# A gate accumulator moved from a PSUM bank to its own SBUF tile, with the freed bank given to the pool of products and convolution

## The chip, the cores and the metric

The kernel runs on one core of one Trainium2 chip. The metric is the device time of one execution in microseconds. The engines that matter here are PE (matrix multiply, output to PSUM only), DVE (vector), ACT (scalar and copies), POOL (elementwise on SBUF) and SP (issues most of the DMAs). All engines run their own instruction streams in order and wait for each other by semaphores. PSUM has eight banks of 512 float32 values on each of 128 partitions; SBUF is the large on-chip memory that all the other tiles lie in.

## The reference

```python
# x: (8, 4224, 192); weight: (8 heads, 7 taps); conv_w: (5, 192); w_val, w_out: (192, 192)
w = softmax(weight)                              # per head, over its 7 taps
x = causal_depthwise_conv(x, w)                  # 7 taps, one filter for each group of 24 channels
gate_pre = sum(conv_w[k] * xp[:, k:k+S] for k in range(5))   # causal, a filter for each channel
gate = 1 / (1 + exp(-gate_pre))
out = (gate * (x @ w_val)) @ w_out
```

Everything is float32.

## The kernel before

Channels lie on partitions and tokens along the free axis. 192 channels don't fit in 128 partitions, so the two halves of the batch are processed side by side in three chunks: chunks 0 and 1 hold 128 channels of each half (tile `x1`, 128 x 2 x m), and chunk 2 holds the remaining 64 channels of both halves (tile `x2`, 128 x m). The tokens are cut into 36 steps of up to m = 502 tokens (24 of them have 502, eight have 448).

The first convolution is done on PE against a banded matrix (`conv_unit`, line 312), copied out of PSUM by ACT (line 321) and rearranged by DMAs into `x1` and `x2`. For each step n the main loop (lines 571 to 598) then does this:

- **The gate.** `gate_open` (ACT, line 382) writes the first of the five taps into an accumulator; `gate_taps` (DVE, line 389) adds four more, each in place: accumulator = x * tap + accumulator; `gate_close` (ACT, line 402) takes the sigmoid. Chunks 0 and 1 share a two-bank PSUM accumulator `pa` (up to 1004 values a partition), chunk 2 has a one-bank PSUM accumulator `pb` (up to 502). The sigmoids go to the SBUF tiles `g1` and `g2`. The profile calls both of these `g`.
- **The first product.** `diagonal`, `main`, `columns` and `rows` (lines 445, 455, 483, 468) form v = x @ w_val in three PSUM banks taken from the pool `ps`.
- **Gating.** `gated` (DVE, line 502) multiplies v from PSUM by the gate, into `g1` or `g2`.
- **Splitting.** To multiply float32 at speed, each operand is split in a rounded part and a remainder: `split1` and `split2` (ACT casts in lines 410 and 418, POOL subtractions in lines 411 and 419). They make `xh`, `xl` from x, and `ph`, `pl` from the gated product. POOL's `pl` of line 411 is that of chunks 0 and 1, and that of line 419 is chunk 2's.
- **The second product** has the same functions with "o", and `project` (ACT, line 518) copies it out.

The pool `ps` serves the products and the banded convolution: five banks before, beside two for `pa` and one for `pb`, which are all eight. The order of instructions on every engine is written out by hand: it is the order of the calls in the loop. In a step DVE does the last two `pa` taps of gate n+1, gating of chunk 2 of step n, gating of chunks 0 and 1, the four `pb` taps of gate n+1, and the first two `pa` taps of gate n+2. POOL does `xl` of step n+1 (lines 411, 419), then `pl` of chunk 2 (line 419) and of chunks 0 and 1 (line 411) of step n.

Of the kernel before, what the change touches and what calls it, by code (L numbers as in the profile page):

```python
# [7 lines left out]
F32 = mybir.dt.float32  # L8
# [5 lines left out]
PSUM = bass.MemoryType.PSUM  # L14
# [62 lines left out]
MB = 502  # L77
# [22 lines left out]
def kernel(  # L100
# [16 lines left out]
    gp = ctx.enter_context(tc.tile_pool(name="gp", bufs=2))  # L117
    pp = ctx.enter_context(tc.tile_pool(name="pp", bufs=2))
    op = ctx.enter_context(tc.tile_pool(name="op", bufs=3))
    ps_g = ctx.enter_context(tc.tile_pool(name="ps_g", bufs=1, space=PSUM))  # L120
    ps_h = ctx.enter_context(tc.tile_pool(name="ps_h", bufs=1, space=PSUM))
    ps = ctx.enter_context(tc.tile_pool(name="ps", bufs=5, space=PSUM))
    ctx.enter_context(
        tc.manual_schedule(engines={ENG.PE, ENG.Activation, ENG.DVE, ENG.Pool, ENG.SP})
    )
# [237 lines left out]
    def views(n, k=KG - 1):  # L363
        g, o, m = STEPS[n]
        b = second(NJS[g])
        x1v = x1s[g][:, : 2 * b].rearrange("p (a t) -> p a t", a=2)
        return x1v[:, :, o + k : o + k + m], x2s[g][:, o + k : o + k + m]
# [3 lines left out]
    accs, g1s, g2s, xs, pr, ots, banks = {}, {}, {}, {}, {}, {}, {}  # L371

    def gate_open(n, i):
        if n >= N:
            return
        m = STEPS[n][2]
        if i == 0:
            acc = ps_g.tile([128, 2, 512], F32, tag="pa", name=f"pa_{n}")[:, :, :m]
        else:
            acc = ps_h.tile([128, 512], F32, tag="pb", name=f"pb_{n}")[:, :m]  # L380
        accs[n, i] = acc
        nc.scalar.mul(acc, views(n, 0)[i], cwt[:, i, 0:1])  # L382

# [10 lines left out]
    def gate_close(n, i):  # L394
        if n >= N:
            return
        m = STEPS[n][2]
        if i == 0:
            dst = g1s[n] = gp.tile([128, 2, MB], F32, tag="g1", name=f"g1_{n}")[:, :, :m]
        else:  # L400
            dst = g2s[n] = gp.tile([128, MB], F32, tag="g2", name=f"g2_{n}")[:, :m]
        nc.scalar.activation(dst, accs.pop((n, i)), AF.Sigmoid)  # L402


# [150 lines left out]
    conv(3)  # L555
    zeros(WARM[2])
    gate_open(0, 0)
    gate_open(0, 1)
    split(0)
    w_out.join(nc.gpsimd)  # L560
    gate_taps(0, 0)
    conv(1)
    gate_close(0, 0)
    gate_open(1, 0)
    w_out.cast(nc.gpsimd)
    conv(first_unit[LAG] - done[0])
    gate_taps(0, 1)
    gate_close(0, 1)
    gate_open(1, 1)

    for n in range(N + 1):
        diagonal("v", n)
        gate_taps(n + 1, 0, 1, 3)
        split(n + 1)
        diagonal("o", n - 1)
        main("v", n, 0)
        main("v", n, 1)
        gate_taps(n + 1, 0, 3, KG)
        columns("v", n)
        gated(n, 2)  # L580
        gate_close(n + 1, 0)
        gate_open(n + 2, 0)
        columns("o", n - 1)
        split_gated2(n)
        project(n - 1, 2)
        rows("v", n)
        gated(n, 0)
        gated(n, 1)
        rows("o", n - 1)
        split_gated1(n)  # L590
        main("o", n - 1, 0)
        gate_taps(n + 1, 1)
        project(n - 1, 0)
        main("o", n - 1, 1)
        project(n - 1, 1)
        conv(todo[n])
        gate_close(n + 1, 1)
        gate_open(n + 2, 1)
# [90 lines left out]
```

## Time and profile before

| | |
|---|---|
| median of 3 runs (range) | 393.77 us (392.7 to 394.51) |
| profiled execution, its own time | 391.79 us |
| span of the profiled execution, first to last instruction | 390.0 us |
| mean granted clock of PE | 0.990 |
| HBM read and written | 29.34 MB, 26.00 MB |

The profiled execution lies 0.5% under the median, and 1.79 us of its time lie outside the span. A "busy" PE in these tables need not be at its peak, since matmuls are pipelined and their ends are modelled. In a row of groups the columns are: line, engine, operation, output and inputs by the program's names, partitions x elements, count, then busy time and mean duration of one in ns, then the idle time of the engine just ahead of these instructions and what ended it. A row of a timeline has start and length in us; "x4" there is four instructions in a row, with the length from the first one's start to the last one's end.

### The profile page before, as it was taken

How to read it: one execution, taken by the hardware profiler on the slowest of the kernel's cores; microseconds unless marked ns; L12 is line 12 of the kernel's file. 1: busy time of each engine (PE TensorE's matmuls, PEld its weight loads, DVE VectorE, ACT ScalarE, POOL GpSimd, SP SyncE). 2: the span in 40 equal slices, each digit the busy share in tenths (PEclk: the TensorE clock that was granted, in tenths of full speed). 3: DMA queues.
4: the chain of work that ended last, by engine and by line, in shares of the span. 5: the costliest groups of instructions: out<-in, count | busy, mean ns of one | idle time of the engine just before them, and what ended most of it. 6: DMA issues, size and time to landing. Idle time of an engine off the chain costs nothing.

```text
span 390.0 us, 8633 instructions
## 1 busy us (share of the span) xinstructions
PE 377.6 (97%) x3204; PEld 322.4 (83%) x3204; DVE 343.5 (88%) x432; ACT 323.7 (83%) x525; POOL 254.6 (65%) x178
## 2 busy tenths in 40 slices
PE   8778999999999999999999999999999999999895
PEld 8768989988888888888888888888888777888684
DVE  5897797888998998998999899899899999999971
ACT  5668798988888888888889888888888888887873
POOL 1968665566667665666666676666566776776781
PEclk9988999999999999999999999999999999999999
DMA  8876779998787688777767768758887644334223
GB/s 301 227 194 206 210 222 281 248 278 258 251 248 217 180 258 248 220 216 244 236 188 242 229 191 260 210 184 265 251 231 218 224 153 154 115 119 151 81 106 145
DMA packets 38226, 82.49 MB, mean 212 GB/s; under 512 B 4841, under 2 KB 17513, under 8 KB 38185
## 3 DMA queue, kind: packets, MB, share of 16 engines
q1 hardware_dynamic: 36936, 80.06, 66.7%
q0 software_dynamic: 960, 1.39, 1.5%
q8 instruction: 25, 0.41, 0.5%
q10 hardware_dynamic: 288, 0.50, 0.4%
q14 instruction: 17, 0.13, 0.1%
HBM read 29.34 MB, written 26.00 MB: 142 GB/s over the span
## 4 chain that ended last, share of the span: by engine, by line
PE 78%; DVE 11%; DMA 4%; ACT 3%; issue 2%; SPq 0%; POOL 0%; DVEq 0%; ACTq 0%
PE pc L312 22%; PE o L455 11%; PE v L455 10%; PE v L483 7%; PE v L468 6%; PE o L483 6%; PE o L468 5%; DVE pa L389 5%; PE v L445 5%; PE o L445 5%; DVE pb L389 3%; DMA x<-xw 3%; DVE g L502 2%; PE pw L204 1%; DMA x<-e 1%
## 5 line engine op out<-in xcount | busy, mean ns | idle before, releaser
L389 DVE SCALAR_TENSOR_TENSOR pa<-x,cwt,pa 128x1004 f32<-128x1004 f32 (+5 forms) x144 | 172.9, 1201 | 5.1 <-ACT pa L382 1.3
L411 POOL TENSOR_TENSOR xl<-x,xh 128x1004 fp32r<-128x1004 f32 (+5 forms) x36 | 74.7, 2075 | 75.4 <-ACT xh L410 67.8
L312 PEld LDWEIGHTS pc<-band,x 128*120 128x120 f32 x912 | 103.3, 187 | 8.4 <-DMA x<-xw 3.6
L312 PE MATMUL pc<-band,x 128*120 128x122 f32 x912 | 104.8, 272 | 5.3 <-DMA x<-xw 5.3
L389 DVE SCALAR_TENSOR_TENSOR pb<-x,cwt,pb 128x502 f32<-128x502 f32 (+5 forms) x144 | 102.3, 710 | 3.8
L502 DVE TENSOR_TENSOR g<-v,g 128x502 f32<-128x502 f32 (+5 forms) x108 | 66.0, 643 | 24.3 <-PE v L468 16.2
L411 POOL TENSOR_TENSOR pl<-g,ph 128x1004 fp32r<-128x1004 f32 (+5 forms) x36 | 79.3, 2201 | 8.3 <-ACT ph L410 6.4
L402 ACT ACTIVATE g<-pa 128x1004 f32<-128x1004 f32 (+5 forms) x36 | 34.5, 958 | 41.9 <-DVE pa L389 20.3
L419 POOL TENSOR_TENSOR pl<-g,ph 128x502 fp32r<-128x502 f32 (+5 forms) x36 | 42.9, 1191 | 37.0 <-ACT ph L418 37.0
L321 ACT COPY e<-pc 120x488 f32<-120x488 f32 x114 | 59.2, 588 | 6.1 <-PE pc L312 5.8
L518 ACT COPY ot<-o 128x502 f32<-128x502 f32 (+5 forms) x108 | 55.8, 551 | 1.2 <-PE o L455 0.7
L382 ACT ACTIVATE pa<-x,cwt 128x1004 f32<-128x1004 f32 (+5 forms) x36 | 37.8, 1050 | 6.7 <-DMA x<-e 4.9
L419 POOL TENSOR_TENSOR xl<-x,xh 128x502 fp32r<-128x502 f32 (+5 forms) x36 | 41.8, 1162 | 0.1
L483 PEld LDWEIGHTS v<-x,wvf 128*64 128x64 f32 x576 | 29.0, 136 | 11.8 <-issue 11.4
L483 PE MATMUL v<-x,wvf 128*64 128x126 f32 (+5 forms) x576 | 37.1, 270 | 0.0
L410 ACT CAST ph<-g 128x1004 fp32r<-128x1004 f32 (+5 forms) x36 | 35.1, 976 | 1.2 <-DVE g L502 1.2
L483 PE MATMUL o<-g,wof 128*64 128x126 f32 (+5 forms) x576 | 35.5, 264 | 0.0
L410 ACT CAST xh<-x 128x1004 fp32r<-128x1004 f32 (+5 forms) x36 | 34.6, 962 | 0.0
L483 PEld LDWEIGHTS o<-g,wof 128*64 128x64 f32 x576 | 30.8, 136 | 0.1
L455 PE MATMUL o<-ph,woh 128*128 128x502 f32 (+5 forms) x72 | 30.8, 428 | 0.0
L455 PE MATMUL v<-xh,wvl 128*128 128x502 f32 (+5 forms) x72 | 27.1, 376 | 0.0
L455 PE MATMUL v<-xh,wvh 128*128 128x502 f32 (+5 forms) x72 | 27.0, 376 | 0.0
(75 smaller groups left out, 574.7 us busy)
## 6 DMA issues: line engine op xcount, KB each, us to landing
x<-xw SPq DMA_DIRECT2D x64, 300.0 KB
out<-ot SPq DMA_DIRECT2D x24, 753.0 KB
x<-e SPq DMA_DIRECT2D x40, 285.9 KB
x<-xw SPq DMA_DIRECT2D x20, 360.0 KB
out<-ot SPq DMA_DIRECT2D x8, 672.0 KB
x<-e SPq DMA_DIRECT2D x32, 141.6 KB
x<-e SPq DMA_DIRECT2D x25, 171.6 KB
x<-e SPq DMA_DIRECT2D x16, 94.4 KB
```

Of the source, the lines that this page charges most:

```text
L312: nc.tensor.matmul(pc[:M, k * WIN : (k + 1) * WIN], lhsT=xtiles[i][:, c : c + M], rhs=band[:, 4 * q + hi, :], start=True, stop=True,)
L321: nc.scalar.copy(e[:, a : a + w], pc[:M, :w])
L389: nc.vector.scalar_tensor_tensor(out=acc, in0=views(n, k)[i], scalar=cwt[:, i, k : k + 1], in1=acc, op0=ALU.mult, op1=ALU.add,)
L410: nc.scalar.copy(h, x)
L411: nc.gpsimd.tensor_tensor(out=l, in0=x, in1=h.bitcast(F32), op=ALU.subtract)
L419: nc.gpsimd.tensor_tensor(out=l, in0=x, in1=h.bitcast(F32), op=ALU.subtract)
L445: nc.tensor.matmul(acc, lhsT=a[:, r], rhs=b, start=(i == 0), stop=False)
L455: nc.tensor.matmul(acc, lhsT=a[:, r], rhs=b[:, q], start=(fresh and i == 0), stop=(not fresh and i == 2))
L468: nc.tensor.matmul(acc, lhsT=a[p, r], rhs=b[p], start=(fresh and i == 0), stop=(not fresh and i == 2))
L483: nc.tensor.matmul(acc[p, c], lhsT=w.f[:, W12 : W12 + 64], rhs=x[:, q, c], start=False, stop=(i == 3),)
L502: nc.vector.tensor_tensor(out=v, in0=banks.pop(("v", n, q)), in1=v, op=ALU.mult)
L518: nc.scalar.copy(ots[n][:, q * m : (q + 1) * m], banks.pop(("o", n, q)))
```

## The change

Chunk 2's gate is no longer summed in a PSUM bank. `gate_open` allocates `g2` itself in SBUF and writes the first tap there, `gate_taps` adds the other four in place in that tile, and the sigmoid of `gate_close` runs in place. The pool of one bank for `pb` goes, and the pool `ps` has six banks. `pa` stays in PSUM.

```diff
-    ps_h = ctx.enter_context(tc.tile_pool(name="ps_h", bufs=1, space=PSUM))
-    ps = ctx.enter_context(tc.tile_pool(name="ps", bufs=5, space=PSUM))
+    ps = ctx.enter_context(tc.tile_pool(name="ps", bufs=6, space=PSUM))
...
         if i == 0:
             acc = ps_g.tile([128, 2, 512], F32, tag="pa", name=f"pa_{n}")[:, :, :m]
         else:
-            acc = ps_h.tile([128, 512], F32, tag="pb", name=f"pb_{n}")[:, :m]
+            acc = gp.tile([128, MB], F32, tag="g2", name=f"g2_{n}")[:, :m]
         accs[n, i] = acc
         nc.scalar.mul(acc, views(n, 0)[i], cwt[:, i, 0:1])
...
         if i == 0:
             dst = g1s[n] = gp.tile([128, 2, MB], F32, tag="g1", name=f"g1_{n}")[:, :, :m]
         else:
-            dst = g2s[n] = gp.tile([128, MB], F32, tag="g2", name=f"g2_{n}")[:, :m]
+            dst = g2s[n] = accs[n, i]
         nc.scalar.activation(dst, accs.pop((n, i)), AF.Sigmoid)
```

No instruction is added or removed, and on no engine does one change its place: all five streams are the same but for the tile names and the waits (and line numbers, which are one lower). Three things differ in the waits. The pool `gp` has two buffers of `g2`, and the buffer is now taken when the gate is opened, not when it is closed, so ACT's opening of chunk 2 waits for POOL's subtraction (line 419) on the gate two before, where it waited for nothing but ACT itself; gating no longer waits for POOL in chunk 2; and PE waits for other releases of banks, since there are six to go round.

ACT before, at the end of step 7 (closing of chunk 2 of gate 8, opening of gate 9, the casts of x, closing and opening of chunks 0 and 1):

```order
L402 ACTIVATE g2_8_1366<-pb_8_1249 128x502 [waits DVE_49]
L382 ACTIVATE pb_9_1368<-x2_4_817,cwt_156 128x502 [waits Activation_49]
L410 CAST xh_9_1376<-x1_4_816 128x1004
L418 CAST xh2_9_1380<-x2_4_817 128x502
L402 ACTIVATE g1_9_1407<-pa_9_1290 128x1004 [waits DVE_49,PE_49,Pool_49]
L382 ACTIVATE pa_10_1409<-x1_4_816,cwt_156 128x2x502 [waits Activation_49]
```

The same place after:

```order
L401 ACTIVATE g2_8_1238<-g2_8_1238 128x502 [waits DVE_49]
L381 ACTIVATE g2_9_1356<-x2_4_810,cwt_153 128x502 [waits Pool_49]
L409 CAST xh_9_1364<-x1_4_809 128x1004
L417 CAST xh2_9_1368<-x2_4_810 128x502
L401 ACTIVATE g1_9_1395<-pa_9_1279 128x1004 [waits DVE_49,PE_49,Pool_49]
L381 ACTIVATE pa_10_1397<-x1_4_809,cwt_153 128x2x502 [waits Activation_49]
```

Nothing moved; the opening of chunk 2 waits for POOL, and both operands of the closing are one SBUF tile.

DVE before, in step 8 (the taps of chunk 2, the taps of chunks 0 and 1 and the gating that follows them):

```order
L389 SCALAR_TENSOR_TENSOR pb_9_1368<-x2_4_817,cwt_156,pb_9_1368 128x502 [waits Activation_49]
L389 SCALAR_TENSOR_TENSOR pb_9_1368<-x2_4_817,cwt_156,pb_9_1368 128x502 [waits DVE_49] x3
L389 SCALAR_TENSOR_TENSOR pa_10_1409<-x1_4_816,cwt_156,pa_10_1409 128x2x502 [waits Activation_49]
L389 SCALAR_TENSOR_TENSOR pa_10_1409<-x1_4_816,cwt_156,pa_10_1409 128x2x502 [waits DVE_49] x3
L502 TENSOR_TENSOR g2_9_1499<-v_9_2_1503,g2_9_1499 128x502 [waits PE_49,Activation_49,Pool_49]
```

The same place after:

```order
L388 SCALAR_TENSOR_TENSOR g2_9_1356<-x2_4_810,cwt_153,g2_9_1356 128x502 [waits Activation_49]
L388 SCALAR_TENSOR_TENSOR g2_9_1356<-x2_4_810,cwt_153,g2_9_1356 128x502 [waits DVE_49] x3
L388 SCALAR_TENSOR_TENSOR pa_10_1397<-x1_4_809,cwt_153,pa_10_1397 128x2x502 [waits Activation_49]
L388 SCALAR_TENSOR_TENSOR pa_10_1397<-x1_4_809,cwt_153,pa_10_1397 128x2x502 [waits DVE_49] x3
L501 TENSOR_TENSOR g2_9_1356<-v_9_2_1490,g2_9_1356 128x502 [waits PE_49,Activation_49]
```

The four taps of chunk 2 now read both their tensors from SBUF and write to SBUF; the taps of chunks 0 and 1 still have theirs in PSUM.

## The prediction

> **What bounds the kernel now.** I read the busy times first, then the chain that ended last, the busy times by stretch, one step of the timeline, and the waits. From the page:
>
> ```profile
> PE 377.6 (97%) x3204; PEld 322.4 (83%) x3204; DVE 343.5 (88%) x432; ACT 323.7 (83%) x525; POOL 254.6 (65%) x178
> ...
> PE 78%; DVE 11%; DMA 4%; ACT 3%; issue 2%; SPq 0%; POOL 0%; DVEq 0%; ACTq 0%
> PE pc L312 22%; PE o L455 11%; PE v L455 10%; PE v L483 7%; PE v L468 6%; PE o L483 6%; PE o L468 5%; DVE pa L389 5%; PE v L445 5%; PE o L445 5%; DVE pb L389 3%; DMA x<-xw 3%; DVE g L502 2%; PE pw L204 1%; DMA x<-e 1%
> ```
>
> PE carries 78% of the chain, DVE 11%, of which the taps of chunk 2 (`pb`) are 3%. By stretch (columns: stretch, length, busy time of PE, weight loads, DVE, ACT, POOL with counts, then clock and DMA):
>
> ```profile
> 0.00:40.00 40.00, 33.47 (x274) 31.90 (x275) 30.82 (x66) 27.36 (x53) 27.04 (x42) 0.91 0.77 227
> 40.00:100.00 60.00, 60.00 (x556) 53.56 (x556) 51.05 (x62) 50.99 (x87) 37.33 (x25) 1.00 0.87 256
> 100.00:200.00 100.00, 100.00 (x836) 84.98 (x837) 92.36 (x106) 88.01 (x139) 65.98 (x39) 1.00 0.73 222
> 200.00:300.00 100.00, 100.00 (x845) 84.35 (x845) 92.35 (x104) 86.62 (x136) 64.75 (x38) 1.00 0.77 231
> 300.00:345.00 45.00, 44.53 (x348) 35.70 (x345) 43.58 (x52) 39.31 (x61) 31.57 (x20) 1.00 0.46 153
> 345.00:390.00 45.00, 39.62 (x354) 31.95 (x353) 33.37 (x47) 31.44 (x56) 27.97 (x19) 0.99 0.35 130
> ```
>
> In the middle PE has no idle time that the profile shows, and DVE is 92% busy: a step is PE's, and DVE has about 0.8 us to spare in each 10.3 us. From 300 on DVE is busier (97%) and the chain passes through it. So whatever lengthens DVE's work in a step by more than 0.8 us sets the step. One step, on DVE and then on POOL:
>
> ```profile
> 164.32 3.08 DVE L389 SCALAR_TENSOR_TENSOR pb<-x,cwt,pb 128x502 f32<-128x502 f32 x4
> 167.30 5.17 DVE L389 SCALAR_TENSOR_TENSOR pa<-x,cwt,pa 128x1004 f32<-128x1004 f32 x4
> 172.38 0.68 DVE L502 TENSOR_TENSOR g<-v,g 128x502 f32<-128x502 f32 x1
> 173.46 1.27 DVE L502 TENSOR_TENSOR g<-v,g 128x502 f32<-128x502 f32 x2 [0.41 <-PE v L468]
> 174.65 3.08 DVE L389 SCALAR_TENSOR_TENSOR pb<-x,cwt,pb 128x502 f32<-128x502 f32 x4
> ```
>
> ```profile
> 162.78 1.28 POOL L419 TENSOR_TENSOR xl<-x,xh 128x502 fp32r<-128x502 f32 x1
> 165.06 1.26 POOL L419 TENSOR_TENSOR pl<-g,ph 128x502 fp32r<-128x502 f32 x1 [1.00 <-ACT ph L418]
> 166.52 2.33 POOL L411 TENSOR_TENSOR pl<-g,ph 128x1004 fp32r<-128x1004 f32 x1 [0.21 <-ACT ph L410]
> 171.03 2.15 POOL L411 TENSOR_TENSOR xl<-x,xh 128x1004 fp32r<-128x1004 f32 x1 [2.18 <-ACT xh L410]
> ```
>
> The reader should see the coincidence: the four `pb` taps (164.32 to 167.40) run while POOL does chunk 2's `pl` (165.06 to 166.32) and starts the large one (166.52). It recurs in every step, because `pl` can begin only when the gating just ahead of the taps is done.
>
> **The change, part by part.**
>
> *The taps get shorter.* The nearest rows: a tap with its accumulator in PSUM, and DVE operations with both tensors in SBUF, all of them from the setup.
>
> ```profile
> L389 DVE SCALAR_TENSOR_TENSOR pb<-x,cwt,pb 128x448 f32<-128x448 f32 x32 | 22.0, 687 | 0.8
> L389 DVE SCALAR_TENSOR_TENSOR pb<-x,cwt,pb 128x502 f32<-128x502 f32 x96 | 71.3, 743 | 2.6
> L389 DVE SCALAR_TENSOR_TENSOR pa<-x,cwt,pa 128x1004 f32<-128x1004 f32 x96 | 121.6, 1267 | 2.5
> L283 DVE TENSOR_TENSOR wvl<-wvf,wvh 128x448 fp32r<-128x448 f32 x1 | 0.6, 625 | 0.7 <-ACT wvh L282 0.7
> L229 DVE TENSOR_TENSOR band<-band,rs 128x488 f32<-128x488 f32 x2 | 1.3, 667 | 1.0 <-ACT band L221 1.0
> ```
>
> At 448 elements SBUF alone takes 625 ns against 687: 62 ns less. The slope is the same, (667 - 625)/40 = 1.05 ns an element against (1267 - 743)/502 = 1.04. So 144 taps save 144 x 0.062 = 8.9 us of DVE, and a step's four 0.25 us.
>
> *The sixth bank.* What PE waited for a bank in all: ahead of `v` in line 445, for ACT's copy out.
>
> ```profile
> PEld v L445 <- ACT ot L518: 0.2, 1, 0.2
> ```
>
> The bank is worth 0.2 us at the most. I take nothing: PE's rows have no gap in the middle for it to fill.
>
> *ACT.* A 502-element copy takes 578 ns out of PSUM (`ot`) and a cast 597 to 606 ns out of SBUF (`ph`, `xh`), so the sigmoid out of SBUF may cost some 30 ns more, 36 x 0.03 = 1.1 us in all. Writing the first tap to SBUF is bounded by the same 30 ns, up or down. ACT has 66 us idle in the span and lies on 3% of the chain; taken at nothing, at worst 2 us. The new wait of ACT for POOL ends early: chunk 2's `pl` of that buffer ends at 166.32, and ACT opens the next gate at 169.26, behind the closing, which itself waits for the last tap.
>
> ```profile
> L518 ACT COPY ot<-o 128x502 f32<-128x502 f32 x72 | 39.0, 578 | 0.0
> L418 ACT CAST ph<-g 128x502 fp32r<-128x502 f32 x24 | 14.3, 597 | 0.0
> L418 ACT CAST xh<-x 128x502 fp32r<-128x502 f32 x24 | 14.6, 606 | 0.0
> 169.26 0.68 ACT L382 ACTIVATE pb<-x,cwt 128x502 f32<-128x502 f32 x1
> ```
>
> *Two engines that read SBUF twice.* This is the price that decides, and no row shows it. Today a DVE tap in the loop reads one tensor from SBUF and one from PSUM, and POOL doesn't disturb it: taps beside POOL and taps without it average 687, 743 and 1267 ns for 448, 502 and 1004 elements, which lie on one line. The last DVE operation with two SBUF tensors ends in the setup before POOL's first subtraction starts:
>
> ```profile
> 15.77 0.56 DVE L249 SCALAR_TENSOR_TENSOR scr<-scr,scr 128x384 f32<-128x384 uint32 x1
> 18.52 0.84 POOL L419 TENSOR_TENSOR xl<-x,xh 128x304 fp32r<-128x304 f32 x1
> ```
>
> After the change there are four such DVE operations in each step, just beside `pl`. What the rows say of the paths: DVE takes two values from SBUF in 1.05 ns, so it has two ways in, and with a PSUM accumulator it needs only one of them. POOL needs (2339 - 1258)/502 = 2.15 ns for each element of two inputs, 1.08 ns a value: the rate of one way in.
>
> ```profile
> L411 POOL TENSOR_TENSOR pl<-g,ph 128x1004 fp32r<-128x1004 f32 x24 | 56.1, 2339 | 5.0 <-ACT ph L410 3.7 <-DMA x<-e 0.6 <-PE pc L312 0.6
> L419 POOL TENSOR_TENSOR pl<-g,ph 128x502 fp32r<-128x502 f32 x24 | 30.2, 1258 | 25.9 <-ACT ph L418 25.9
> ```
>
> The lower bound is no cost: the paths are separate, and DVE only gains 8.9 us. The upper bound is that DVE's second way in and POOL's one are the same and go to one instruction at a time, from its start to its end. I take that end, since it is the reading in which the numbers fit one shared path (a PSUM accumulator leaves POOL untouched, POOL has exactly one path's rate), and keep the other for the range.
>
> The Trainium skill, "SBUF — State Buffer", section "Who interferes with whom", says that a DVE instruction with two SBUF inputs contends with a GpSimd instruction that reads SBUF, that the shared pair is an exclusive lock, and that whichever starts second "fully blocks" until the first is done. No run here shows it yet; by that rule the sum is the one below, and without it the sum ends some 87 us lower.
>
> *The sum.* In a step of 502: the taps start. Tap 2 ends, and `pl` of chunk 2, ready 0.7 us after the taps began, goes first: tap 3 waits 1.26 us. By then ACT has cast chunks 0 and 1, so the large `pl` is ready, and in the gap after tap 3 it goes ahead of tap 4: 2.33 us. POOL's `xl` doesn't collide, because its casts stand on ACT behind the closing of chunk 2, which waits for the last tap; it has the 5.08 us of `pa` taps and the gating to finish. DVE's step is then 2.98 - 0.25 (167.30 - 164.32, less the saving) + 5.08 (172.38 - 167.30) + 0.68 + 1.19 (174.65 - 173.46) = 9.68 us of work and 3.59 of waiting: 13.27 us against 10.33 (174.65 - 164.32). PE (10.33) and ACT (under 10) then have slack, and DVE no longer waits for PE.
>
> ```profile
> L411 POOL TENSOR_TENSOR pl<-g,ph 128x1004 fp32r<-128x1004 f32 (+5 forms) x36 | 79.3, 2201 | 8.3 <-ACT ph L410 6.4
> L419 POOL TENSOR_TENSOR pl<-g,ph 128x502 fp32r<-128x502 f32 (+5 forms) x36 | 42.9, 1191 | 37.0 <-ACT ph L418 37.0
> ```
>
> For the whole span: all `pl` is 122.2 us; the last step's 1.9 us (a small block, no taps beside it) don't count, which leaves 120.3. DVE's busy time 343.5 - 8.9 + 120.3 = 454.9. DVE's idle time between 40 and 345 (305 - 279.3 = 25.7 us) is swallowed; that of the start and the end (9.2 + 11.6) stays: 475.7 us of span. With the 1.8 us outside it, 477.5 us against this execution's 391.79. The execution lies 0.5% under the median of 393.77; scaled to that, 479 us.
>
> **The rivals.**
>
> *Sharing by halves.* DVE and POOL interleave on the shared path, value by value. Then a tap beside POOL reads its second tensor at half rate: 67,700 elements in all 144 taps x 1.05 ns = 71 us more. 343.5 - 8.9 + 71 + 20.8 + 1.8 = 428 us, and with some taps free of POOL, 415. For it: POOL's port is nearly full, but not quite. Against it: DVE and POOL would have to be arbitrated for each value.
>
> *DVE keeps the path* (the other side: not slower). The gap between two taps is some 0.03 us (3.08 us for four of 743 ns). If that is too short for POOL to get in, all four taps run through, and POOL begins `pl` at 164.32 + 2.73 + 0.1 = 167.15 and ends it at 168.41. PE needs it at 168.85, the third matmul of `o` in line 445:
>
> ```profile
> 168.85 0.39 PE L445 MATMUL o<-pl,woh 128*128 128x502 f32 x1
> ```
>
> POOL has 3.3 us idle in a step and makes good the 2.1 us. The time is that of before, 391 to 397 us. It decides if POOL can't start within 0.03 us of a tap's end. It loses again where `pl` is ready ahead of the first tap.
>
> *No contention.* The saving counts only where `pb` taps are on the chain: 3% of 390 = 11.7 us x 62/743 = 1.0 us. 390 to 394 us. The same holds if the change is judged by its bank: 0.2 us. It would be the case if POOL has its own way in.
>
> **How the numbers follow.** One at a time: 0.62. Sharing by halves: 0.19. DVE keeps the path: 0.09. No contention: 0.10. The predicted time is the first case's, 479 us. Its own range is 460 (only the 2.15 ns an element of `pl` blocks, not the fixed 0.2 us of each of 71) to 500 (0.1 us lost at each of 72 handovers, and half of the 25.7 us of idle time not swallowed). The range takes in the second case: 415 to 500, which leaves out 0.19. This kernel's runs spread by 0.46%, so 0.5% is about what can be told from no change. Slower by over 0.5%: the first two cases and 0.4 of the third, 0.85. Faster: a third of the last, 0.03. Within: 0.12.
>
> **What would show it.** If right: the rows of the chunk-2 taps (line 388) no longer all alike, about half near 0.68 us and the others longer by 1.3 and 2.3, or idle time of DVE of that size ahead of them; POOL's `pl` rows of their old length, some begun later; steps of 13.3 us; DVE in place of PE on most of the chain; PE's busy share well under 90%, with waits for DVE's gating; ACT idle ahead of the closing of chunk 2. Each part: single undisturbed taps of 0.68 us; ACT's sigmoid of chunk 2 within 0.03 us of 0.63. Sharing by halves would show all taps beside POOL at 1.2 us and longer `pl`. DVE keeping the path would show taps of 0.68 in a row and `pl` always after them. The prediction is wrong if taps and `pl` overlap at their old lengths: then there is no shared path, and the time is that of before.

## The result and the profile after

The changed kernel takes 461.18 us (median of 6 runs, 460.47 to 462.25) against 394.08 us for the kernel before (6 runs, 392.7 to 395.9). The ratio is 1.170, with a 95% interval of 1.167 to 1.174: 67 us slower. 479 us had been forecast, with a range of 415 to 500. The profiled execution has a span of 459.9 us.

The busy times and the chain of the changed kernel, from its page:

```profile
PE 397.5 (86%) x3204; PEld 320.6 (70%) x3204; DVE 435.7 (95%) x432; ACT 322.4 (70%) x525; POOL 271.2 (59%) x178
...
DVE 67%; issue 12%; ACT 6%; DMA 4%; PE 4%; POOL 3%; SPq 1%; DVEq 0%; ACTq 0%; POOLq 0%
DVE g L388 32%; DVE pa L388 23%; DVE g L501 11%; DMA x<-e 4%; ACT g L401 1%; SPq L347 1%; PE v L454 1%; POOL x L347 1%; DMA band<-bw 1%; POOL pl L418 1%; ACT pa L381 1%; ACT e L320 1%; PE o L482 1%; PE v L482 1%; ACT ph L417 1%
```

DVE's busy time grew from 343.5 to 435.7 us though it has the same 432 instructions, and the chain changed hands: PE from 78% to 4%, DVE from 11% to 67%. The groups with the same elements as before (of the changed kernel, shapes kept together on the page; lines are one lower):

```profile
L388 DVE SCALAR_TENSOR_TENSOR g<-x,cwt,g 128x502 f32<-128x502 f32 (+5 forms) x144 | 197.8, 1374 | 3.8
L388 DVE SCALAR_TENSOR_TENSOR pa<-x,cwt,pa 128x1004 f32<-128x1004 f32 (+5 forms) x144 | 172.7, 1200 | 5.3 <-ACT pa L381 1.4
...
L418 POOL TENSOR_TENSOR pl<-g,ph 128x502 fp32r<-128x502 f32 (+5 forms) x36 | 46.8, 1301 | 79.6 <-ACT ph L417 77.2
L410 POOL TENSOR_TENSOR pl<-g,ph 128x1004 fp32r<-128x1004 f32 (+5 forms) x36 | 91.5, 2541 | 1.7 <-ACT ph L409 0.5
```

The taps of chunk 2 went from 102.3 us (710 ns each) to 197.8 us (1374 ns): 95.5 us more, in their own rows and not as idle time ahead of them. The taps of chunks 0 and 1, whose accumulators stayed in PSUM, still take 1200 ns. POOL's two `pl` groups also got longer, by 3.9 and 12.2 us. An average hides how that comes about; the timeline of one step, tap by tap, shows it. First the four taps of chunk 2 on DVE, then what POOL did, then what follows on DVE:

```profile
197.46 0.73 DVE L388 SCALAR_TENSOR_TENSOR g<-x,cwt,g 128x502 f32<-128x502 f32 x1
198.22 0.74 DVE L388 SCALAR_TENSOR_TENSOR g<-x,cwt,g 128x502 f32<-128x502 f32 x1
199.00 1.62 DVE L388 SCALAR_TENSOR_TENSOR g<-x,cwt,g 128x502 f32<-128x502 f32 x1
200.66 2.72 DVE L388 SCALAR_TENSOR_TENSOR g<-x,cwt,g 128x502 f32<-128x502 f32 x1
```

```profile
198.71 1.37 POOL L418 TENSOR_TENSOR pl<-g,ph 128x502 fp32r<-128x502 f32 x1 [2.50 <-ACT ph L417]
200.11 2.72 POOL L410 TENSOR_TENSOR pl<-g,ph 128x1004 fp32r<-128x1004 f32 x1
205.68 2.16 POOL L410 TENSOR_TENSOR xl<-x,xh 128x1004 fp32r<-128x1004 f32 x1 [2.85 <-ACT xh L409]
```

```profile
203.29 5.17 DVE L388 SCALAR_TENSOR_TENSOR pa<-x,cwt,pa 128x1004 f32<-128x1004 f32 x4
208.37 1.85 DVE L501 TENSOR_TENSOR g<-v,g 128x502 f32<-128x502 f32 x3
210.14 5.93 DVE L388 SCALAR_TENSOR_TENSOR g<-x,cwt,g 128x502 f32<-128x502 f32 x4
```

Taps 1 and 2 are undisturbed. POOL's `pl` starts at 198.71, during tap 2. Tap 3 ends at 200.62, 0.54 us after that `pl` (200.08), and tap 4 at 203.38, 0.55 us after the large `pl` (202.83). DVE held up POOL in turn: the large `pl`, which starts while tap 3 runs, takes 2.72 us against 2.34 before, and the small one, which starts during tap 2, 1.37 against 1.26. The step is 210.14 - 197.46 = 12.68 us, against 10.33 before. The pattern 0.73, 0.74, 1.62, 2.72 recurs to within 0.02 us from about 120 to 400 us, and from about 60 us on the last two taps of a step are always the long ones, but for the last step.

### The profile page after: what moved, and what is told of

It is laid out like the page before. It is cut to its first block, busy times and chain, and to the rows that moved or that the text cites. A ratio compares the mean times of both kernels' runs of the same rounds, so it can differ in the third digit from the quotient of the medians.

```text
span 459.9 us, 8673 instructions
## 1 busy us (share of the span) xinstructions
PE 397.5 (86%) x3204; PEld 320.6 (70%) x3204; DVE 435.7 (95%) x432; ACT 322.4 (70%) x525; POOL 271.2 (59%) x178
## 4 chain that ended last, share of the span: by engine, by line
DVE 67%; issue 12%; ACT 6%; DMA 4%; PE 4%; POOL 3%; SPq 1%; DVEq 0%; ACTq 0%; POOLq 0%
DVE g L388 32%; DVE pa L388 23%; DVE g L501 11%; DMA x<-e 4%; ACT g L401 1%; SPq L347 1%; PE v L454 1%; POOL x L347 1%; DMA band<-bw 1%; POOL pl L418 1%; ACT pa L381 1%; ACT e L320 1%; PE o L482 1%; PE v L482 1%; ACT ph L417 1%
## 5 line engine op out<-in xcount | busy, mean ns | idle before, releaser
L388 DVE SCALAR_TENSOR_TENSOR g<-x,cwt,g 128x502 f32<-128x502 f32 (+5 forms) x144 | 197.8, 1374 | 3.8
L311 PE MATMUL pc<-band,x 128*120 128x122 f32 x912 | 110.8, 279 | 39.6 <-DVE g L501 32.3
L418 POOL TENSOR_TENSOR pl<-g,ph 128x502 fp32r<-128x502 f32 (+5 forms) x36 | 46.8, 1301 | 79.6 <-ACT ph L417 77.2
L410 POOL TENSOR_TENSOR pl<-g,ph 128x1004 fp32r<-128x1004 f32 (+5 forms) x36 | 91.5, 2541 | 1.7 <-ACT ph L409 0.5
L501 DVE TENSOR_TENSOR g<-v,g 128x502 f32<-128x502 f32 (+5 forms) x108 | 63.1, 639 | 1.4 <-PE v L467 0.6
L320 ACT COPY e<-pc 120x488 f32<-120x488 f32 x114 | 58.1, 592 | 4.1 <-PE pc L311 4.0
L401 ACT ACTIVATE g<-g 128x502 f32<-128x502 f32 (+5 forms) x36 | 21.7, 602 | 37.3 <-DVE g L388 37.3
```

What stands on the lines that cost most here:

```text
L311: nc.tensor.matmul(pc[:M, k * WIN : (k + 1) * WIN], lhsT=xtiles[i][:, c : c + M], rhs=band[:, 4 * q + hi, :], start=True, stop=True,)
L320: nc.scalar.copy(e[:, a : a + w], pc[:M, :w])
L388: nc.vector.scalar_tensor_tensor(out=acc, in0=views(n, k)[i], scalar=cwt[:, i, k : k + 1], in1=acc, op0=ALU.mult, op1=ALU.add,)
L410: nc.gpsimd.tensor_tensor(out=l, in0=x, in1=h.bitcast(F32), op=ALU.subtract)
L418: nc.gpsimd.tensor_tensor(out=l, in0=x, in1=h.bitcast(F32), op=ALU.subtract)
L501: nc.vector.tensor_tensor(out=v, in0=banks.pop(("v", n, q)), in1=v, op=ALU.mult)
```

## Experiments

The theory: a DVE instruction that takes two tensors from SBUF and a POOL instruction that reads SBUF exclude each other, one instruction at a time. The rivals: the redistributed banks and changed waits; taps that are slow because they write or read back in SBUF; a sharing of the path by values. The baseline is the kernel before on the same chip: 393.78 us for `five_banks`, `pool_writes_only`, `pool_in_pieces` and `tap_immediate`, 393.66 us for the other four.

**Is it the bank?** The changed kernel with the sixth bank taken away again.

```diff
-    ps = ctx.enter_context(tc.tile_pool(name="ps", bufs=6, space=PSUM))
+    ps = ctx.enter_context(tc.tile_pool(name="ps", bufs=5, space=PSUM))
```

> The changed kernel with five banks in the pool of products and convolution instead of six, one PSUM bank left empty. If the loss comes from the taps of chunk 2 and POOL taking turns at reading SBUF, the bank has no part in it: 461 us, within 1%, and the third and fourth tap of a step at 1.6 and 2.7 us again. If the new allocation of banks or the changed waits of PE cost the time, it returns to 394 to 400 us.

464.21 us, ratio 1.180 (1.177 to 1.183). The 502-element taps average 1448 ns, as with six banks (1452).

```profile
L388 DVE SCALAR_TENSOR_TENSOR g<-x,cwt,g 128x502 f32<-128x502 f32 x96 | 139.0, 1448 | 2.6
```

The loss needs no sixth bank. With the bank the ratio is 1.170 (1.167 to 1.174), some 3 us less, and those intervals don't meet. That the bank is the reason is not shown: the granted clock was 0.94 to 0.95 here and 0.98 with the bank, and the two profiled executions, 461.84 and 461.71 us, hardly differ.

**Which side of the tap costs?** Two kernels on the base of the one before: in the first the taps read the PSUM accumulator and write SBUF; in the second they read SBUF twice and write PSUM.

```diff
+            g2s[n] = gp.tile([128, MB], F32, tag="g2", name=f"g2_{n}")[:, :m]
...
-                out=acc, in0=views(n, k)[i], scalar=cwt[:, i, k : k + 1],
+                out=acc if i == 0 else g2s[n], in0=views(n, k)[i], scalar=cwt[:, i, k : k + 1],
...
-            dst = g2s[n] = gp.tile([128, MB], F32, tag="g2", name=f"g2_{n}")[:, :m]
+            dst = accs[n, i] = g2s[n]
```

> The kernel before, but the four taps of chunk 2 write to the SBUF tile of the gate, while they still read the accumulator from its PSUM bank (so only the first and the last tap are in the sum; the other taps are left out of it). If reading two tensors from SBUF is what makes taps and POOL take turns: taps of 743 ns, no turns, 392 to 396 us. If writing the accumulator to SBUF is what costs: taps of 1.6 and 2.7 us, 455 to 465 us.

```diff
+            g2s[n] = gp.tile([128, MB], F32, tag="g2", name=f"g2_{n}")[:, :m]
...
-        nc.scalar.mul(acc, views(n, 0)[i], cwt[:, i, 0:1])
+        nc.scalar.mul(acc if i == 0 else g2s[n], views(n, 0)[i], cwt[:, i, 0:1])
...
-                in1=acc, op0=ALU.mult, op1=ALU.add,
+                in1=acc if i == 0 else g2s[n], op0=ALU.mult, op1=ALU.add,
...
-            dst = g2s[n] = gp.tile([128, MB], F32, tag="g2", name=f"g2_{n}")[:, :m]
+            dst = g2s[n]
```

> The mirror image: the taps of chunk 2 read both tensors from SBUF (the accumulator as ACT opened it) and write to the PSUM bank, five banks in the pool (again only the first and the last tap are in the sum). If the second read from SBUF takes turns with POOL: third and fourth tap 1.6 and 2.7 us, 455 to 465 us, though nothing is written to SBUF. If the write to SBUF costs: 392 to 396 us.

The groups of the first and then of the second (output <- inputs: `g` is SBUF, `pb` PSUM):

```profile
L390 DVE SCALAR_TENSOR_TENSOR g<-x,cwt,pb 128x502 f32<-128x502 f32 x96 | 70.6, 736 | 2.6
```

```profile
L390 DVE SCALAR_TENSOR_TENSOR pb<-x,cwt,g 128x502 f32<-128x502 f32 x96 | 139.2, 1450 | 2.5
```

Writing to SBUF costs nothing: 736 ns, 393.21 us, ratio 0.999 (0.997 to 1.001). Reading the accumulator from SBUF costs all of it, with nothing written to SBUF: 1450 ns, 464.21 us, ratio 1.179 (1.177 to 1.181). The loss is in the second read. (The taps that read PSUM run beside the same POOL subtractions and aren't disturbed.)

**Is it POOL's reading?** The changed kernel, in which POOL hardly reads at the critical place but still writes there (shown for chunk 2; chunks 0 and 1 are done alike).

```diff
-        nc.gpsimd.tensor_tensor(out=l, in0=x, in1=h.bitcast(F32), op=ALU.subtract)
+        c = slice(0, 4 if tag == "p" else m)
+        nc.gpsimd.tensor_tensor(out=l[:, c], in0=x[:, c], in1=h.bitcast(F32)[:, c], op=ALU.subtract)
+        if tag == "p":
+            for _ in range(2):
+                nc.gpsimd.memset(l.bitcast(F32)[:, 4:], 0.0)
```

> The changed kernel, but POOL's remainder of the gated product reads only the first 4 columns of each chunk and sets the other columns to zero with two memsets (the remainder is left out of the second product). POOL still starts at the same place and writes for about as long, but hardly reads. Turns at the read path: no tap waits longer than about 0.3 us, all four taps near 0.73 us, and 393 to 402 us. If taps with an SBUF accumulator are slow for another reason (their own write and read back, or POOL's presence as such): taps of 1.6 and 2.7 us stay, 450 to 465 us.

One step, DVE and then POOL (the large remainder's two memsets are the last row):

```profile
194.51 3.07 DVE L388 SCALAR_TENSOR_TENSOR g<-x,cwt,g 128x502 f32<-128x502 f32 x4
```

```profile
195.29 0.20 POOL L423 TENSOR_TENSOR pl<-g,ph 128x4 fp32r<-128x4 f32 x1 [1.14 <-ACT ph L421]
195.43 1.08 POOL L426 MEMSET pl<- 128x498 f32 x2
196.69 0.20 POOL L411 TENSOR_TENSOR pl<-g,ph 128x8 fp32r<-128x8 f32 x1 [0.18 <-ACT ph L409]
196.84 1.92 POOL L414 MEMSET pl<- 128x996 f32 x2
```

With the accumulator in SBUF, four taps take 3.07 us again, straight across POOL's writes. 392.32 us, ratio 0.997 (0.994 to 0.999). So it takes both: a second SBUF read on DVE and an SBUF read on POOL. Where POOL does read, in `xl`, which is left as it was, a tap still waits: one of 448 elements, early in the run, takes 4.20 us (see the end). The run also bounds what the change is worth without the collision: at most 0.6%, with POOL's work mostly left out.

**Does one input on POOL suffice?** POOL copies the rounded part in place of subtracting.

```diff
-        nc.gpsimd.tensor_tensor(out=l, in0=x, in1=h.bitcast(F32), op=ALU.subtract)
+        if tag == "p":
+            nc.gpsimd.tensor_copy(out=l, in_=h.bitcast(F32))
+        else:
+            nc.gpsimd.tensor_tensor(out=l, in0=x, in1=h.bitcast(F32), op=ALU.subtract)
```

> The changed kernel with POOL's remainder of the gated product replaced by a copy of the rounded part (the remainder is left out, the copy stands in its place): one input from SBUF in place of two, started at the same place. If any POOL instruction that reads SBUF holds the read path from start to end, taps three and four wait for a copy each, less 0.33 us that overlap in the measured turns: with copies of about 0.7 and 1.3 us 410 to 430 us. If only POOL instructions with two inputs block: 392 to 397 us.

404.59 us in one run, and in the groups:

```profile
L411 POOL CAST pl<-ph 128x1004 fp32r<-128x1004 f32 x24 | 25.0, 1041 | 14.7 <-ACT ph L409 13.9 <-PE pc L311 0.8
L422 POOL CAST pl<-ph 128x502 fp32r<-128x502 f32 x24 | 18.9, 789 | 41.4 <-ACT ph L420 28.2 <-PE pc L311 13.0 <-PE o L460 0.2
```

```profile
L388 DVE SCALAR_TENSOR_TENSOR g<-x,cwt,g 128x502 f32<-128x502 f32 x96 | 96.6, 1006 | 2.6
```

The taps average 1006 ns, so a POOL instruction with one SBUF input blocks too. The time lies under the 410 to 430 us expected. The two copies took 0.79 and 1.04 us, not 0.7 and 1.3: 0.17 us less in a step, some 6 us in 36 steps, which is about what is missing to 410.

The fourth tap of a step, and the large copy:

```profile
224.59 1.60 DVE L388 SCALAR_TENSOR_TENSOR g<-x,cwt,g 128x502 f32<-128x502 f32 x1
```

```profile
224.63 1.03 POOL L411 CAST pl<-ph 128x1004 fp32r<-128x1004 f32 x1 [0.62 <-ACT ph L409]
```

The tap's row starts 0.04 us ahead of the copy's, and it is the tap that waits: it ends 0.53 us after the copy. Which of two goes first can't be read from so small a difference of their starts.

**For how long is the path held?** POOL's two subtractions cut into six (shown for chunks 0 and 1; that of chunk 2 is cut in two).

```diff
-        nc.gpsimd.tensor_tensor(out=l, in0=x, in1=h.bitcast(F32), op=ALU.subtract)
+        hf = h.bitcast(F32)
+        if tag == "p":
+            for q in range(2):
+                for c in (slice(0, m // 2), slice(m // 2, m)):
+                    nc.gpsimd.tensor_tensor(out=l[:, q, c], in0=x[:, q, c], in1=hf[:, q, c], op=ALU.subtract)
+        else:
+            nc.gpsimd.tensor_tensor(out=l, in0=x, in1=hf, op=ALU.subtract)
```

> The changed kernel with POOL's remainder of the gated product cut into six subtractions of at most 251 elements a partition in place of one of 502 and one of 1004: the same elements, about 0.8 us more of POOL's time in a step. If the read path is given up at the end of each POOL instruction, taps three and four wait for one piece each, some 0.4 us: 394 to 402 us. If POOL keeps it as long as its next instruction is ready, tap three waits for all pieces (about 4 us) and tap four for none: 480 to 510 us.

Four taps of one step, then the first three pieces on POOL:

```profile
198.82 0.73 DVE L388 SCALAR_TENSOR_TENSOR g<-x,cwt,g 128x502 f32<-128x502 f32 x1
199.59 0.74 DVE L388 SCALAR_TENSOR_TENSOR g<-x,cwt,g 128x502 f32<-128x502 f32 x1
200.37 1.08 DVE L388 SCALAR_TENSOR_TENSOR g<-x,cwt,g 128x502 f32<-128x502 f32 x1
201.48 1.10 DVE L388 SCALAR_TENSOR_TENSOR g<-x,cwt,g 128x502 f32<-128x502 f32 x1
```

```profile
200.08 0.83 POOL L426 TENSOR_TENSOR pl<-g,ph 128x251 fp32r<-128x251 f32 x1 [1.55 <-ACT ph L423]
200.87 1.17 POOL L426 TENSOR_TENSOR pl<-g,ph 128x251 fp32r<-128x251 f32 x1
202.01 1.17 POOL L414 TENSOR_TENSOR pl<-g,ph 128x251 fp32r<-128x251 f32 x1
```

399.91 us, ratio 1.017 (1.014 to 1.020). A tap waits for one piece, 0.35 us, and the next piece waits for the tap: in these steps the turns go strictly by instruction. The same elements read by POOL cost 6 us in place of 67. The taps are through after two short turns, with 0.35 + 0.35 = 0.70 us lost in a step, and DVE has 0.8 us to spare in a step of the kernel before, so the time shows little of it. That speaks against a sharing by values, in which the number of pieces wouldn't matter.

**Does it scale?** All gates summed in SBUF.

```diff
-    gp = ctx.enter_context(tc.tile_pool(name="gp", bufs=2))
+    gp = ctx.enter_context(tc.tile_pool(name="gp", bufs=3))
...
-            acc = ps_g.tile([128, 2, 512], F32, tag="pa", name=f"pa_{n}")[:, :, :m]
+            acc = gp.tile([128, 2, MB], F32, tag="g1", name=f"g1_{n}")[:, :, :m]
...
-            dst = g1s[n] = gp.tile([128, 2, MB], F32, tag="g1", name=f"g1_{n}")[:, :, :m]
+            dst = g1s[n] = accs[n, i]
```

> The changed kernel with the gates of chunks 0 and 1 summed in their SBUF tile too (three buffers of each gate tile; no PSUM accumulators left). If each of POOL's four subtractions of a step now falls among DVE's eight taps and takes one turn, less 0.33 us each: DVE waits 7.0 - 1.3 = 5.7 us in a step in place of 2.9, steps of 15.6 us, 545 to 570 us. If only chunk 2's taps are disturbed: about 461 us.

546.75 us in one run. A step on DVE (eight taps, then gating), and POOL's four subtractions in it:

```profile
264.33 13.46 DVE L387 SCALAR_TENSOR_TENSOR g<-x,cwt,g 128x502 f32<-128x502 f32 x8
277.71 1.84 DVE L500 TENSOR_TENSOR g<-v,g 128x502 f32<-128x502 f32 x3
279.48 3.15 DVE L387 SCALAR_TENSOR_TENSOR g<-x,cwt,g 128x502 f32<-128x502 f32 x3
```

```profile
265.38 1.57 POOL L417 TENSOR_TENSOR pl<-g,ph 128x502 fp32r<-128x502 f32 x1 [3.80 <-ACT ph L416]
266.92 2.79 POOL L409 TENSOR_TENSOR pl<-g,ph 128x1004 fp32r<-128x1004 f32 x1
272.56 2.17 POOL L409 TENSOR_TENSOR xl<-x,xh 128x1004 fp32r<-128x1004 f32 x1 [2.85 <-ACT xh L408]
274.70 2.03 POOL L417 TENSOR_TENSOR xl<-x,xh 128x502 fp32r<-128x502 f32 x1
```

The step is 279.48 - 264.33 = 15.15 us against 15.6 expected. POOL's `xl`, harmless in the changed kernel, now takes its turns as well.

**Where the forecast saving of 62 ns a tap was.** The kernel before, with a constant in place of the weight.

```diff
-                out=acc, in0=views(n, k)[i], scalar=cwt[:, i, k : k + 1],
+                out=acc, in0=views(n, k)[i], scalar=(cwt[:, i, k : k + 1] if i == 0 else 0.5),
```

> The kernel before, with the four DVE taps of chunk 2 multiplied by the constant 0.5 instead of the per-channel weight read from SBUF (the gate of chunk 2 is another one). The prediction took the 62 ns by which such a tap is longer than a setup operation with both tensors in SBUF for the price of PSUM. If it is the price of the weight operand, the 502-element taps fall from 743 to about 680 ns with their accumulator still in PSUM; if it is PSUM's, they stay at 743. The time stays at that of before, 390 to 396 us, since PE sets the step.

```profile
L389 DVE SCALAR_TENSOR_TENSOR pb<-x,pb 128x502 f32<-128x502 f32 x96 | 65.6, 684 | 2.5
```

684 ns with the accumulator in PSUM, 390.61 us in one run, in which the weights are left out. The 59 ns belong to the weight operand.

No version here points to a kernel faster than the one before: without the collision, six banks come to 392.3 us with POOL's work mostly left out, and of the versions that sum the gate in SBUF and keep all the work none does better than 399.9.

## Why the prediction was right, and which terms were off

- **The bound moved from PE to DVE, by turns at the read path.** Shown: it needs DVE's second SBUF read (`sbuf_in_only`, `sbuf_out_only`) and POOL's read (`pool_writes_only`), it goes by instructions (`pool_in_pieces`), and the likeliest case of the four was the right one. By the rule of the Trainium skill ("SBUF — State Buffer", section "Who interferes with whom") quoted in the prediction, the second to start waits for the first: the trace agrees in kind, with tap 4 ending 0.55 us after POOL, but by the rows of `pool_one_input` a tap that starts 0.04 us before POOL waits too.
- **The place.** In a step, taps 3 and 4 were to wait for chunk 2's `pl` and the large one, `xl` was not to collide, and PE was to wait for gating; so it was, but for the first steps (one early tap waits for `xl`) and the last. Two of the signs that were named did not come: the undisturbed taps are not 0.68 us long, and POOL's `pl` rows are longer than before. PE's share is 86%, and its waits for gating ahead of the convolution are 32.3 us in 27 places:

```profile
PE pc L311 <- DVE g L501: 32.3, 27, 2.0
```

- **The wait was sized too large: 120.3 us, measured 95.5.** A step's 1.26 + 2.33 = 3.59 us came to (1.62 - 0.74) + (2.72 - 0.74) = 2.86. The term took both instructions in their full length. But a tap needs only 0.54 us after POOL's end, not 0.74, so 0.20 us of it runs beside POOL; and the large `pl` is longer by 0.38 us where it waited 0.51 (from 200.11 to 200.62), so 0.13 us of POOL's start runs beside the tap. Two turns of 0.33 us are 0.66 of the missing 0.73, and the rest is the 0.03 us between two taps, in which POOL gets ahead. The prediction's own lower end, 460 us, allowed 0.2 us for each of 71 instructions, 14.2 us in all; that is 465 from 479, and not 460. (Scaled as it says, the forecast itself is 480.) The measured 461.18 us lies below what that end was built on.
- **The saving of 8.9 us did not exist.** The undisturbed 502-element taps take 0.73 to 0.74 us in SBUF, and took 0.743 in PSUM: a hundredth of a microsecond less at most, where 0.062 was forecast. The step that failed compared a tap, which reads a weight for each partition, with setup operations that read none; `tap_immediate` shows the difference on that operand. The row to compare with was there in the profile before: gating reads PSUM without such an operand, and its 676 ns at 502 elements lie within 6 ns of the line through the setup operations (625 at 448, 667 at 488):

```profile
L502 DVE TENSOR_TENSOR g<-v,g 128x502 f32<-128x502 f32 x72 | 46.5, 676 | 12.1 <-PE v L468 11.3 <-POOL xl L411 0.4
```

- **The sum.** Taps 95.5 in place of -8.9 + 120.3 = 111.4: -15.9 us. The two errors offset each other in part, which is luck: without the saving the same sum would have come to 479 + 8.9 = 488 us. Gating's busy time is 2.9 us shorter (66.0 to 63.1): it no longer waits for PE, and its rows now follow one another and overlap. DVE's idle time is 459.9 - 435.7 = 24.2 us where 20.8 were expected. The forecast span of 475.7 less 15.9 and about 3.3 for the rest of DVE's work, plus 3.4, is 459.9.
- **The small terms.** ACT's sigmoid of chunk 2 takes 623 ns at 502 elements where it took 627, and the opening in SBUF 700 where it took 684: both within the 30 ns. At 448 elements both are just over it (601 for 567, 677 for 639). The new wait of ACT for POOL doesn't show. No run tries the sixth bank alone; `pool_writes_only`, which has it, is within 0.6% of the kernel before.
- **The rivals.** Sharing by halves would have shown taps of 1.2 us and a `pl` slowed throughout, and is excluded by tap 4's 2.72 us (half rate would add only 502 x 1.05 ns = 0.53 us to 0.74) and by the pieces. DVE keeping the path is excluded by tap 3: POOL got in between two taps some 0.03 us apart. No contention is excluded by the result.

## What to carry to other kernels

Before an accumulator goes from PSUM to SBUF, ask whether the DVE instruction then has two SBUF inputs, and what POOL reads at that moment: here the two took turns by whole instructions, and what DVE lost in each turn was POOL's instruction less some 0.35 us. Where they must meet, short POOL instructions lose far less than long ones: 0.70 us of a step against 2.86 for the same elements, and with DVE's spare time 6 us against 67. And compare durations only between rows with the same kinds of operands: a per-partition weight alone was 59 ns.

## What was not expected of the hardware

- The waiting shows as the length of the instruction, not as idle time ahead of it. DVE reads 95% busy while it waits for 95 us; a busy share alone would call it a saturated engine.
- One early tap waited for several POOL instructions in a row, and what let them all go first is open. It starts during the last of POOL's DMA issues and ends 0.49 us after the third subtraction behind them:

```profile
38.34 4.97 DVE L388 SCALAR_TENSOR_TENSOR g<-x,cwt,g 128x448 f32<-128x448 f32 x1
```

```profile
37.18 1.65 POOL L347 DMA_DIRECT2D x<-e  x3
38.85 2.10 POOL L410 TENSOR_TENSOR xl<-x,xh 128x896 fp32r<-128x896 f32 x1
40.91 1.14 POOL L418 TENSOR_TENSOR xl<-x,xh 128x448 fp32r<-128x448 f32 x1
42.00 0.82 POOL L418 TENSOR_TENSOR pl<-g,ph 128x302 fp32r<-128x302 f32 x1
```

  Turns after each instruction would have let it in at 40.95. It recurs at the same place in two other runs: in `pool_writes_only` a tap of 4.20 us from 37.62 waits for both `xl` subtractions, and in `pool_in_pieces` one of 3.32 us from 41.37 waits for the end of `xl` and four pieces. POOL's DMA issues as such don't hold the path: the tap ahead of the one in `pool_writes_only` runs beside them at its usual 0.68 us. Nor is it enough that the subtractions are ready, since in the regular steps of `pool_in_pieces` two pieces that wait for the same cast are parted by a tap. The cause wasn't found.
